# Two attention blocks on one core: the order of PE's work from a written list, part of the wide matmuls as column tiles, eps sums on GpSimd, and the last job's two copies from separate tiles

## The chip, the cores and the metric

The kernel runs on one core of a Trainium2 chip. The metric is device time of one execution in microseconds; the times given are the median of several runs. Engines are named as in the profile: PE (TensorE matmul) and PEld (its weight loads), DVE (VectorE), ACT (ScalarE), POOL (GpSimd), SP (SyncE, which issues most transfers).

## What is computed

Two attention blocks over 2048 tokens of width 640, 32 heads of 20, side by side in the output. Block A works in four segments of 512 tokens: causal softmax attention inside the segment, mixed by a gate per head with a read of a memory that earlier segments have filled. Block B is sliding-window attention (256 keys back).

```
# A, per segment s
p = softmax(qs ks^T * Dh**-0.5 + causal mask);  a_dot = p vs
num = phi(qs) M ;  den = phi(qs) z + 1e-06 ;  a_mem = num / den      # phi(t) = t+1 if t>0 else exp(t)
o = g * a_mem + (1-g) * a_dot
M += phi(ks)^T vs ;  z += sum(phi(ks))
# B
p = softmax(where(0 <= i-j < 256, q k^T * Dh**-0.5, -1e9));  o = p v
# both: out = concat over heads(o) @ wo
```

## The kernel before

**Chunks.** The work is eight chunks of 512 tokens in the order A0, B0, A1, B1, ... A3, B3, numbered n = 0 to 7. For each chunk, PE makes queries and keys (`qk_job`: ten chains of five matmuls of 512 columns), values (`v_job`: eight chains of five matmuls of 320 columns), scores, value sums and, at the end, the output projection (`final_job`: eight chains of five matmuls of 320 columns). A chain accumulates in one of two PSUM banks (`bank`, tiles m0 and m1), and a copy on DVE empties the bank (L488, L664, L669, L1014). These chains go through `wide` (L855): one matmul on the whole 128 x 128 array per step.

**Visits.** A score batch (`score_batch`, L733) fills two score tiles of three (`sc`, two banks each), with matmuls of 20 rows that run four or eight at a time as row tiles (L745). ACT turns the two tiles into `pt` by an exp each (L761). Masks follow, on POOL (`affine_select`, L800) or on DVE (multiplication with `ends`, L778). There are 153 batches. A batch can be written when the first exp of the batch before has read its tile. I call a visit what PE does from one batch to the next: the batch, then pieces of chains and, mostly, one value sum.

**Value sums.** `av` (L805, L814) and, in the last chunk, `av_tile` (L823, L835) multiply `pt` with the values of four heads in four column tiles of 32 that run side by side. Each value tile carries a column of ones, so that the sum's divisor comes out beside it. `turn` (L861) transposes the bank on DVE (L870), which frees it; `norm` (L875) takes the reciprocal of the divisor on DVE (L895) and multiplies on POOL (L905) into `o`. For A chunks after the first there is a second product for each group, the read of the memory (`mem`, L843, through `wide`). Its `norm` first adds eps to the divisor (L890, DVE), takes the reciprocal (L893), multiplies on POOL into `u` (L905) and adds `u` to `o` on DVE (L918). There are 24 of these.

**Order.** All engines run their instructions in the written order; the order is made when the kernel is built. Class `Flow` keeps a clock per engine with costs in ns for each operation. The loop in `body` (L1327 to L1422) looks at each step for what is ready by these clocks, in a fixed preference: the next score batch (L1331, not before `room`, a limit of 160 matmuls within 3000 ns, allows it, and not if ACT is far ahead and a job is ready, `may_wait`); the next value sum or memory read from the one queue `pend` (L1362, with a rule that holds it back to avoid a change of form); the next step of a job (L1387). Jobs are generators that yield what they wait for. DVE's work is put in the order of `flush`, with jobs that may wait for an idle moment (`when_idle`: the passes of phi, L523 and L529, half of the DVE masks, reciprocals, adds of `u`).

**Forms of PE.** The model in `on_pe_` charges 97 ns when the form changes ("full", "row", "row64", "col").

**End.** `final` (L928) stores `o` to DRAM and loads it back transposed for the output projection; the last chunk does this for three tiles of 128 tokens. The last 128 tokens are transposed on PE instead (`last_job`, L1023: L1036 and L1041 into the two halves of one `sc` tile), copied by DVE (L1048, 256 columns) and ACT (L1050, 384 columns) and projected by two chains (`last_half`, L1061). This job is put ahead of all others (L1476).

Of the kernel before, what the change touches and what calls it, by code (L numbers as in the profile page):

```python
# [13 lines left out]
P = 128  # L14
# [13 lines left out]
AT = 0  # L28
FETCH = 160
FETCH_NS = 3000  # L30
BACK = 800.0
NTT = 4
QPOOL = 750.0
GAP = 48
# [19 lines left out]
LEAD = 500.0  # L54

# [11 lines left out]
class Flow:  # L67
# [3 lines left out]
    def __init__(self):  # L71
# [15 lines left out]
        self.issued = []  # L87
# [11 lines left out]
    def room(self, n):  # L99


        while self.issued and self.issued[0][0] <= self.pe - FETCH_NS:
            self.issued.pop(0)
        have = n + sum(k for _, k in self.issued)
        t = self.pe
        for t0, k in self.issued:
            if have <= FETCH:
                break
            have -= k
            t = t0 + FETCH_NS  # L110
        return t

    def on_pe(self, mode, ns, cols, ready=0.0, n=1):
        self.issued.append((max(self.pe, ready), n))
        return self.on_pe_(mode, ns, cols, ready)
# [22 lines left out]
    def on_dve(self, ns, ready=0.0):  # L138
        self.dve = max(self.dve, ready) + ns
        return self.dve + 138.0  # L140

    def on_pool(self, ns, ready=0.0):
        self.pool = max(self.pool, ready) + ns
        return self.pool + 98.0
# [68 lines left out]
class _K:  # L213
# [29 lines left out]
    def warm_up(self, z):  # L243

# [211 lines left out]
    def qk_job(self, n, what, pieces, w_ap, dst, needs, scratch, phi=None):  # L456
# [6 lines left out]
        if what == "k" and self.chunks[n][0] == "B":  # L463
            at = SH
            c = self.chunks[n][1]
            if 0 in pieces and c > 0:
                def prefix(t0):
                    nc.vector.tensor_copy(out=dst[:, :, 0:SH],
                                          in_=self.kB[(c - 1) % 2][:, :, L:L + SH])
                    f.on_dve(290.0)  # L470
# [28 lines left out]
    def phi(self, in_, t, m, use):  # L499
# [13 lines left out]
        def one(in_, e, es, m, ta):  # L513
            box = []

            def s1():
# [8 lines left out]
                f.on_dve(300.0, t)  # L525

            def s2():
                r = box[-1]
                nc.vector.tensor_tensor(out=r if len(box) == 1 else e, in0=r, in1=e, op=ALU.min)  # L529
                td = f.on_dve(370.0, ta)  # L530
# [60 lines left out]
    def dm_job(self, seg, pkT, v):  # L591
# [12 lines left out]
        for some in (own, [(lambda kt, h=h: spare[:, kt, R2 * h:R2 * h + R2], R2,  # L604
# [6 lines left out]
            for lhs, rows, xs, g0 in some:  # L611
# [8 lines left out]
                f.on_pe("full", 4 * mm_ns(n), 4 * n)  # L620
# [151 lines left out]
    def mask(self, m, pt, te, ready, x):  # L772
        nc, f = self.nc, self.f
        kind, c0, n = m
        if kind == "ends":
            def go():
# [6 lines left out]
                ready[x] = f.on_dve(72.0 + 1.036 * n, te)  # L783
# [71 lines left out]
    def wide(self, ps, lhsT, rhs, n, start, stop):  # L855

        self.nc.tensor.matmul(ps[:, 0:n], lhsT=lhsT, rhs=rhs, start=start, stop=stop)  # L857
        self.f.on_pe("full", mm_ns(n), n)
        self.f.left = 0 if stop else self.KT - 1 if start else self.f.left - 1
# [15 lines left out]
    def norm(self, turned, dst, add_to, last, g=None):  # L875
# [12 lines left out]
        def s1():  # L888
            if add_to:
                nc.vector.tensor_single_scalar(out=rr[:], in_=tv[:, :, DH], scalar=EPS,  # L890
                                               op=ALU.add)
                f.on_dve(100.0, t0)
                nc.vector.reciprocal(out=rr[:], in_=rr[:])  # L893
            else:
                nc.vector.reciprocal(out=rr[:], in_=tv[:, :, DH])  # L895
            t1 = f.on_dve(276.0, t0)
            f.at(t1 - 100.0, lambda: s2(t1))

        def s2(t1):
# [14 lines left out]
            def add():  # L914
# [4 lines left out]
                t3 = f.on_dve(300.0, t2)  # L919
# [6 lines left out]
        f.when_idle(t0, s1)  # L926

    def final(self, n, o, scr, wo, out2d, r0, col, t0, t1, t):  # L928
# [19 lines left out]
        def turn(tl):  # L948
            if n not in self.oT:
# [3 lines left out]
                else:  # L953
# [7 lines left out]
                                                 lambda: box.get("t"))))  # L961
# [61 lines left out]
    def last_job(self, o, wo, out2d, r0, col, t):  # L1023
# [11 lines left out]
        for b in range(LT):  # L1035
            nc.tensor.matmul(wide[:, b], lhsT=o[:, b0 + b, 0:P], rhs=one, start=True, stop=True,  # L1036
                             skip_group_check=True)
            f.on_pe("full", mm_ns(P), P)
        for j in range(4):
            for b in range(LT):  # L1040
                nc.tensor.matmul(two[HD * j:HD * j + HD, 1, HD * b:HD * b + HD],  # L1041
# [3 lines left out]
        f.on_pe("col", 150.0, 128)  # L1045

        oT = [self.pq[:, 0, 0:2 * P], self.pkT[:, 0, 0:3 * P]]
        nc.vector.tensor_copy(out=oT[0], in_=two[:, 0, 0:2 * P])  # L1048
        td = f.on_dve(330.0, f.seen)
        nc.scalar.copy(out=oT[1], in_=two[:].rearrange("p h c -> p (h c)")[:, 2 * P:5 * P])  # L1050
        ta = f.on_act(400.0, f.seen)
        self.sc_free[own] = max(ta, td)
        yield max(ta, td)
        oT = [oT[m // 2 if m < 4 else 1][:, P * (m % 2 if m < 2 else m - 2):][:, 0:P]
              for m in range(self.KT)]
# [94 lines left out]
    def job(self, gen):  # L1150
        return [gen, next(gen)]
# [29 lines left out]
    def seed(self, n):  # L1181
# [7 lines left out]
        add = lambda gen: self.jobs.append(self.job(gen))  # L1189
# [5 lines left out]
        else:  # L1195
            add(self.dm_job(c - 1, self.pkT, self.vA))
# [7 lines left out]
        for half, pieces in enumerate(((0, 1, 2), (3, 4))):  # L1204
            for some in ([(m,) for m in pieces] if first else [pieces]):
                for what, w, dst, phi in qk:
                    need = [tx, gate] + ([self.known("wB" + what, some[0])] if first else [])
                    add(self.qk_job(n, what, some, w, dst, need, self.scr[what + kind][c], phi))
                if first and some[0] == AT:
                    add(self.late_v())  # L1210
            if first:
                v[3] = v[3] + [self.known("wBv", half)]
            add(self.v_job(n, half, *v))
# [368 lines left out]
```

## Time and profile before

| | us |
|---|---|
| median of 3 runs (lowest, highest) | 335.01 (334.55, 335.17) |
| the profiled execution | 334.66 |
| its span | 332.9 |
| granted TensorE clock | 1.0 |

| engine | busy, us | share of the span | instructions |
|---|---|---|---|
| PE | 317.7 | 95% | 6617 |
| ACT | 302.4 | 91% | 332 |
| DVE | 266.0 | 80% | 556 |
| POOL | 255.7 | 77% | 648 |

The span runs from the first to the last record of the profiled execution; that execution took 334.66 us, 1.8 us more. Busy time is the union of an engine's records. Records of matmuls overlap, and so do those of ACT: a row's mean duration is longer than the distance between two in a row. Lines such as L857 are lines of the kernel before; L857 is the helper `wide`, so its tiles tell which chain it is.

### The profile page before, as it was taken

To read this page: it belongs to the slowest core of one execution; us is meant where nothing else is said; L and a number is where in the kernel's file an instruction comes from. 1 tells how busy PE (TensorE), PEld (TensorE's weight loads), DVE (VectorE), ACT (ScalarE), POOL (GpSimd) and SP (SyncE) were. 2 spreads that over 40 slices of the span, in tenths; PEclk is the share of its full clock that TensorE was granted. 3 is DMA by queue.
4 is the path that set the end of the run, shared out by engine and by line. 5 is a ranking of instruction groups with operands and counts; after the bars stand their busy time and mean duration, and the time that the engine had idled before them with its cause. 6 is when DMAs were issued, how large, how long until landed. Compare 5 with 4: busy or idle time off the path is not lost.

```text
span 332.9 us, 15825 instructions
## 1 busy us (share of the span) xinstructions
PE 317.7 (95%) x6617; PEld 174.1 (52%) x6617; DVE 266.0 (80%) x556; ACT 302.4 (91%) x332; POOL 255.7 (77%) x648
## 2 busy tenths in 40 slices
PE   7999999999999999999999999999999999999996
PEld 2444446554444455546654546455654545666564
DVE  6878667788988899989958898888677898876653
ACT  1879999998999999999999999989999999999841
POOL 8446779987668799984876879996965969977750
PEclk9999999999999999999999999999999999999999
DMA  6975745846566852245699245044584054659762
GB/s 195 397 245 135 194 134 121 177 117 183 127 207 145 182 147 75 47 98 107 167 209 189 65 90 161 2 98 69 136 168 114 14 161 126 154 135 192 169 138 99
DMA packets 76260, 47.36 MB, mean 142 GB/s; under 512 B 48381, under 2 KB 73181, under 8 KB 76189
## 3 DMA queue, kind: packets, MB, share of 16 engines
q1 hardware_dynamic: 75469, 45.71, 56.2%
q8 instruction: 51, 0.84, 1.0%
q10 hardware_dynamic: 720, 0.66, 0.7%
q14 instruction: 20, 0.16, 0.2%
HBM read 17.62 MB, written 16.96 MB: 104 GB/s over the span
## 4 chain that ended last, share of the span: by engine, by line
PE 56%; DVE 16%; ACT 11%; POOL 7%; issue 6%; DMA 2%; SPq 1%; ACTq 0%; DVEq 0%; POOLq 0%
PE m L857 35%; PE sc L745 11%; ACT pt L761 11%; PE m L814 6%; POOL pt L800 4%; DVE pt L778 3%; PE m L835 2%; POOL u L905 2%; DVE tt L870 2%; DVE kA L488 2%; DVE pq L529 2%; DMA beta<-in_A_beta_dram 1%; DVE vA L664 1%; DVE pq L523 1%; DVE ot L1014 1%
## 5 line engine op out<-in xcount | busy, mean ns | idle before, releaser
L761 ACT ACTIVATE pt<-sc 128x1024 bf16<-128x1024 f32 (+2 forms) x306 | 284.8, 1014 | 12.4 <-PE sc L745 10.0
L800 POOL TENSOR_SCALAR_AFFINE_SELECT pt<-pt 128x128 bf16<-128x128 bf16 (+1 forms) x512 | 176.7, 373 | 62.1 <-ACT pt L761 58.4
L870 DVE STREAM_TRANSPOSE tt<-m 128x512 f32<-128x512 f32 x88 | 61.4, 711 | 20.3 <-PE m L814 9.6
L905 POOL TENSOR_TENSOR o<-tt,rr 128x320 bf16<-128x320 f32 x64 | 47.6, 743 | 4.4 <-DVE rr L895 4.1
L857 PEld LDWEIGHTS <-xT 128*128 128x128 bf16 x350 | 32.0, 97 | 25.0 <-issue 13.3
L745 PE MATMUL sc<-qB,kB 20*64 20x64 bf16 (+2 forms) x1728 | 38.6, 218 | 1.2 <-issue 0.7
L778 DVE TENSOR_TENSOR pt<-pt,ends 128x1024 bf16<-128x1024 bf16 (+2 forms) x50 | 36.0, 734 | 0.0
L745 PEld LDWEIGHTS <-kB 20*64 20x64 bf16 (+1 forms) x1728 | 21.6, 98 | 23.3 <-issue 22.0
L745 PE MATMUL sc<-qA,kA 20*64 20x64 bf16 (+4 forms) x1024 | 33.3, 237 | 0.4 <-ACT qA L485 0.2
L1014 DVE CAST ot<-m 128x320 bf16<-128x320 f32 x56 | 26.8, 485 | 7.5 <-PE m L857 7.3
L857 PEld LDWEIGHTS <-oT 128*128 128x128 bf16 x280 | 24.7, 98 | 11.4 <-issue 1.0
L857 PE MATMUL m<-wBv,xT 128*128 128x320 bf16 x160 | 27.0, 299 | 2.4 <-DVE tt L870 2.3
L857 PE MATMUL m<-wv_A,xT 128*128 128x320 bf16 x160 | 26.1, 299 | 2.6 <-DVE vA L664 1.9
L857 PE MATMUL m<-xT,wq_A 128*128 128x512 bf16 x100 | 25.8, 380 | 1.5 <-DVE vA L664 1.0
L857 PE MATMUL m<-xT,wk_A 128*128 128x512 bf16 x100 | 26.0, 388 | 1.1 <-DVE qA L488 0.7
L857 PE MATMUL m<-xT,wBq 128*128 128x512 bf16 x100 | 26.8, 381 | 0.1
L857 PE MATMUL m<-xT,wBk 128*128 128x512 bf16 x100 | 25.9, 381 | 0.0
L745 PEld LDWEIGHTS <-kA 20*128 20x128 bf16 (+1 forms) x1024 | 13.6, 97 | 20.8 <-issue 19.8
L814 PE MATMUL m<-pt,vA 128*32 128x192 bf16 (+3 forms) x512 | 23.7, 275 | 0.0
L857 PE MATMUL m<-wo_A,oT 128*128 128x320 bf16 x140 | 22.7, 300 | 0.2
L488 DVE CAST kB<-m 128x512 bf16<-128x512 f32 x20 | 13.8, 691 | 9.2 <-PE m L857 9.2
L857 PE MATMUL m<-wo_B,oT 128*128 128x320 bf16 x120 | 19.4, 300 | 0.3 <-DVE ot L1014 0.3
(108 smaller groups left out, 405.9 us busy)
## 6 DMA issues: line engine op xcount, KB each, us to landing
out_dram<-ot SPq DMA_DIRECT2D x29, 160.0 KB
scr_o<-o SPq DMA_DIRECT2D x28, 160.0 KB
xT<-in_B_x_dram SPq DMA_DIRECT2D x8, 288.0 KB
xT<-in_A_x_dram SPq DMA_DIRECT2D x8, 256.0 KB
scr_pk<-e SPq DMA_DIRECT2D x15, 128.0 KB
vS<-vA SPq DMA_DIRECT2D x16, 87.0 KB
vL<-vB SPq DMA_DIRECT2D x8, 174.0 KB
scr_kA<-kA SPq DMA_DIRECT2D x16, 60.0 KB
```

The source lines that it names most:

```text
L488: nc.vector.tensor_copy(out=dst[:, m, at:at + L], in_=ps[:, :])
L529: nc.vector.tensor_tensor(out=r if len(box) == 1 else e, in0=r, in1=e, op=ALU.min)
L745: nc.tensor.matmul(ps[j // 2][h0:h1, j % 2, c0:c0 + nq], lhsT=k[rows, g, k0:k0 + h1 - h0], rhs=q[rows, g, q0:q0 + nq], start=True, stop=Tr ...
L761: nc.scalar.activation(out=pt[:, :, lo:hi], in_=ps[i][:, :, lo:hi], func=ACT.Exp, scale=self.scale)
L778: nc.vector.tensor_tensor(out=blk, in0=blk, in1=self.ends[:, c0, :].unsqueeze(1).unsqueeze(1) .to_broadcast([P, 2, n // SH, SH]), op=ALU.mult)
L800: nc.gpsimd.affine_select(out=blk, in_=blk, pattern=pat, compare_op=ALU.is_ge, fill=self.zero, base=base, channel_multiplier=mul)
L814: nc.tensor.matmul(O[HD * j:HD * j + HD, q0:q0 + nq], lhsT=v[:, at_head(h):at_head(h) + HD], rhs=pts[j // 2][:, j % 2, c0:c0 + nq], start= ...
L835: nc.tensor.matmul(O[HD * j:HD * j + HD, o0:o0 + nq], lhsT=v[:, at_head(h):at_head(h) + HD], rhs=pts[j // 2][:, j % 2, c0:c0 + nq], start= ...
L857: self.nc.tensor.matmul(ps[:, 0:n], lhsT=lhsT, rhs=rhs, start=start, stop=stop)
L870: self.nc.vector.transpose(out=tt[:], in_=O[:, :])
L905: nc.gpsimd.tensor_tensor(out=to[:] if add_to else to, in0=a, in1=b, op=ALU.mult)
L1014: nc.vector.tensor_copy(out=ot[:, 320 * hf:320 * hf + 320], in_=ps[:, 0:320])
```

## The change

Four things change, and some costs of the planner's model with them.

1. **A list.** `PLAN` names in order what PE is given: `S` or `s` a score batch, `A` a value sum, `M` a memory read, `k20*6` six matmul steps of the job "keys of chunk 2, from piece 0", `o` an output job, `d` the memory's update, `z` the last job. The loop takes what stands next in the list, as soon as the clocks say that it is ready; the rules of preference hold only where no list is left. Memory reads have a queue of their own (`memq`) and wait for their group's value sum.
2. **Column tiles for chains.** In a visit that begins with a capital `S` and holds an `A`, `wide` issues each matmul as four, one for each 32 columns of the weights, in the form of the value sums.
3. **Eps sums.** The addition of eps to the divisor of the 24 memory reads goes from DVE to POOL (`s0`).
4. **The last job** writes its wide part (four of five pieces, 512 columns) and its tiled part (128 columns) into two `sc` tiles; DVE copies the one and ACT the other. In the list it comes last.

The model in `Flow` now charges for 256 instructions of PE in less than 3000 ns (in place of `room`), lets DVE and POOL hold each other up, and has smaller costs for phi and the adds.

```diff
+PLAN = (
+    "k00*5 q00*5 k01*4 S k01 q01*5 v00*4 s v00*14 S v00*2 k02*2 s k02*3 q02*4 S q02 k03*5 q03*5 "
...
+    "S o00*4 o10*5 S A o10*5 S o10*10 S o10*7 S o10*3 A o10*3 S o10*2 q50*5 S A q50*3 S q50*2 "
...
+    "o50*10 S A o70*5 S o60*9 A o60 S o60*5 S o60*11 S o60*9 S A o60*5 o70*5 o71*5 A o71*5 "
+    "o72*2 z0*4 ")
...
     def wide(self, ps, lhsT, rhs, n, start, stop):
-        self.nc.tensor.matmul(ps[:, 0:n], lhsT=lhsT, rhs=rhs, start=start, stop=stop)
-        self.f.on_pe("full", mm_ns(n), n)
+        f = self.f
+        if self.by_tiles:
+            for j in range(4):
+                s = slice(HD * j, HD * j + HD)
+                self.nc.tensor.matmul(ps[s, 0:n], lhsT=lhsT[:, s], rhs=rhs, start=start,
+                                      stop=stop, tile_position=(0, HD * j),
+                                      skip_group_check=True)
+            f.on_pe("col", n / 2.4 + COL_NS, n, 0.0, 4)
+        else:
+            self.nc.tensor.matmul(ps[:, 0:n], lhsT=lhsT, rhs=rhs, start=start, stop=stop,
+                                  skip_group_check=True)
+            f.on_pe("full", mm_ns(n), n)
...
-        def s1():
+        def s0():
+            nc.gpsimd.tensor_single_scalar(out=rr[:], in_=tv[:, :, DH], scalar=EPS, op=ALU.add)
+            t = f.on_pool(EPS_NS, t0)
+            f.when_idle(t, lambda: s1(t))
+
+        def s1(te=None):
             if add_to:
-                nc.vector.tensor_single_scalar(out=rr[:], in_=tv[:, :, DH], scalar=EPS,
-                                               op=ALU.add)
-                f.on_dve(100.0, t0)
                 nc.vector.reciprocal(out=rr[:], in_=rr[:])
...
-        oT = [self.pq[:, 0, 0:2 * P], self.pkT[:, 0, 0:3 * P]]
-        nc.vector.tensor_copy(out=oT[0], in_=two[:, 0, 0:2 * P])
+        oT = [self.pq[:, 0, 0:4 * P], self.pkT[:, 0, 0:P]]
+        nc.vector.tensor_copy(out=oT[0], in_=two[:, 0, :])
...
+        two = self.ps.tile([P, 2, 512], F32, name="sc", bufs=NSC)
...
-        nc.scalar.copy(out=oT[1], in_=two[:].rearrange("p h c -> p (h c)")[:, 2 * P:5 * P])
+        nc.scalar.copy(out=oT[1], in_=two[:, 0, 0:P])
...
+            want = plan[-1] if plan else None
+            self.by_tiles = bool(plan) and visits[i]
+            if i < len(bs) and want in (None, "S", "s"):
...
-                        if t <= f.pe and not self.may_wait():
+                        if t <= f.pe and (want or not self.may_wait()):
...
+                if want and jb[2] != want and (jb[2][0] != "d" or jb[1] in ("bank", 0.0)):
+                    continue
```

## Prediction, before the changed kernel had run

> **What bounds the kernel now.** I read the page first: engine shares, then the tenths by slice, then the chain that ended last.
>
> ```profile
> PE 317.7 (95%) x6617; PEld 174.1 (52%) x6617; DVE 266.0 (80%) x556; ACT 302.4 (91%) x332; POOL 255.7 (77%) x648
> ...
> PEclk9999999999999999999999999999999999999999
> ...
> q8 instruction: 51, 0.84, 1.0%
> ...
> PE 56%; DVE 16%; ACT 11%; POOL 7%; issue 6%; DMA 2%; SPq 1%; ACTq 0%; DVEq 0%; POOLq 0%
> ```
>
> PE leads the chain, ACT is close behind, and the granted clock is full throughout, so a matmul column has one price. The busy shares of both overstate them, because records overlap. The timeline of 306 to 333 us shows the true spacing:
>
> ```profile
> 305.40 7.47 ACT L761 ACTIVATE pt<-sc 128x1024 bf16<-128x1024 f32 x8
> ...
> 308.91 1.53 PE L857 MATMUL m<-wo_B,oT 128*128 128x320 bf16 x10
> ...
> 310.38 0.40 PE L745 MATMUL sc<-qB,kB 20*128 20x128 bf16 x16
> ...
> 315.41 0.34 PE L745 MATMUL sc<-qB,kB 20*128 20x128 bf16 x11 [0.74 <-issue]
> ...
> 317.15 0.40 PE L745 MATMUL sc<-qB,kB 20*128 20x128 bf16 x16
> ...
> 322.84 0.73 POOL L905 TENSOR_TENSOR o<-tt,rr 128x320 bf16<-128x320 f32 x1 [1.65 <-DVE rr L895]
> ...
> 325.40 0.48 ACT L1050 CAST pkT<-sc 128x384 bf16<-128x384 f32 x1 [2.32 <-DVE pq L1048]
> ...
> 327.57 2.26 PE L857 MATMUL m<-wo_B,xT 128*128 128x320 bf16 x15
> ```
>
> Eight exps of 1024 columns take 7.47 us, the last record 1.03: one every (7.47-1.03)/7 = 0.92 us. Ten wide matmuls of 320 columns take 1.53, a record 0.30: one every 0.136 us, 320/2.4 ns plus 2.7. The ten end their streaming at 308.91+1.36 = 310.27 and the scores begin at 310.38: a **change of form** (wide, row tiles, column tiles) costs 0.1 us. Over all changes in the trace the distance of starts, less the columns, has medians of 91 to 115 ns; I use 97.
>
> I then cut the program at its 153 visits (one score batch, then what PE does until the next). PE's own work is its columns, 2 to 4 ns a group, and 97 ns a change; ACT's is 0.833 ns a column and 52 ns an instruction. From the first score (8.66 us) to the last (317.15) there are 246.4 + 375 x 0.097 = 282.8 us of PE work and 283.9 of ACT work, and it lasts 308.5. Both engines have some 25 us to spare, in different visits: taking the longer of the two, visit by visit, gives 301.9. The other 6.6 us, and more that the visits hide, are PE waiting for PSUM banks. The waits view shows them:
>
> ```profile
> ACT pt L761 <- PE sc L745: 10.0, 24, 1.5
> DVE tt L870 <- PE m L814: 9.6, 25, 0.9
> ...
> PE m L857 <- DVE vA L664: 2.9, 5, 0.8
> ...
> PE m L857 <- DVE tt L870: 2.3, 12, 0.2
> ```
>
> ACT idles 10.0 us for scores and DVE 9.6 for value sums, so neither is the bound throughout; PE in turn waits for DVE's copies and transposes to free a bank. Matmul records hide the first 0.16 us of a wait. By distances of starts, PE's waits for DVE sum to 15.7 us: 5.5 behind transposes (L870), nearly all in the three stages with memory groups (98-137, 176-212, 254-290 us), 4.9 behind value copies (L664).
>
> **The change, part by part.** The profiled execution has a span of 332.9 us (334.66 with what lies around it); the median of the runs is 335.0, so I add 2.1 to a span.
>
> 1. *The list, forms of PE.* Built, the changed kernel has 314 changes of form against 382, and 289 wide matmuls are issued as four column tiles beside value sums. Columns are the same, 250.4 us. From first to last score: 310 changes against 375, -6.3 us; some 4.0 us of output chains come from behind the last score to ahead of it; 289 groups of four at 4 ns instead of 2.5, +0.4. Together 280.9 against 282.8: **-1.9**. The price of a group is bounded by the quartets of L814: 2.7 ns over the columns for 320, 13.3 for 448, so 0 to +3.1.
>
> 2. *The eps sums.* 24 of these leave DVE:
>
> ```profile
> L890 DVE TENSOR_SCALAR rr<-tt 128x16 f32<-128x16 f32 x24 | 8.9, 371 | 0.0
> ```
>
> 24 x 0.371 = 8.9 us of DVE, 3.0 in each memory stage, and they stand between transposes for which PE waits 5.2 us there. What goes is between none and all of that; I take half, **-2.5**. On POOL nothing has this shape; the nearest row is 128x20 at 0.23 (L338), so 24 x 0.23 = 5.5 us more. POOL is already full in part of these stages (busy 7.00 of 7 us at 123-130 and at 130-137), and behind each sum queue masks for which value sums wait. Upper bound: all 5.5 on the path; lower: 0. I take 0, since a list may place value sums later than the masks.
>
> 3. *ACT's cover.* Every visit still has two exps. The list's visits are less even: the longer of PE and ACT, visit by visit, sums to 304.9 against 301.9. A long visit after a short one is partly forgiven: the second exp (0.92) runs while PE proceeds, less score (0.2) and delivery (0.2), so half a us. I take **+1.0**, from 0 to +3.0.
>
> 4. *Instruction supply.* PE gets 867 more weight loads and as many matmuls: 14,970 against 13,236. The 51 instruction transfers are 16 KB each, one per 256 instructions. At 315.41 PE stops in the midst of a batch with nothing to wait for: 0.91 us of distance between two starts. The instructions just before were the densest stretch (370 in 6 us). In the changed list the last 35 us reach 430 to 500 by the same sums. [...] I take one more such stop, **+1.0**, from 0 to +6 (rival B).
>
> 5. *The tail.* Before, the last rows' outputs (last_job) go ahead of 15 other output matmuls, which end PE's work at 329.8; 15.75 us pass from last score to end. The list puts last_job at the end. Its chain, by rows: last score 317.15; product on POOL ends 323.57; 20 transposing matmuls 0.65; a copy of 512 columns 0.69 (row L488) with 0.24 of delivery, instead of 0.42 and 0.48 in turn (ACT's waited for DVE's, 325.40); ten groups 1.36+0.3; from there 3.0 as from the last copy at 329.87 to the end. That is 329.8 against 332.9, -3.1; PE's other work behind the last score is 5.6 us (7.45 less 1.9 of last_job), just under the 6.4 of the chain, so some of it shows. **-2.6**, from 0 to -3.5. The third tile's transposed outputs must be there: before they were issued at 320.04 and used late; the list makes their tile a visit (1.8 us) earlier and needs them about 1 us earlier.
>
> SP's transfers are moved with their stages, none is added. New separate queues for memory groups, and the waiting for the add, only order the same operations.
>
> Sum: -1.9 - 2.5 + 1.0 + 1.0 - 2.6 = **-5.0**: span 327.9, time **330.0**. The terms' ends alone reach from 324 to 343, not all at once.
>
> **Rivals.**
> A. *The waits at the stages' ends go too.* Five stops of 0.6 to 0.9 us behind value and query copies (77.9, 86.3, 143.5, 154.7, 233.4) and many smaller ones make the 10.2 us of waits for DVE outside the transposes. If the order spreads these chains, half goes: 330.0 - 5 = 325. For: ACT could follow, having 25 us to spare. Against: phi's passes on DVE, which those copies queue behind, are unchanged.
> B. *PE starves.* This is the slower side. The stop at 315.41 fits a block lasting some 4.1 us from crossing to use. If blocks drained faster than that always pay the difference, the list's dozen densest (2.6 to 3.9 us by the sums) pay 7.1 against 1.2 before, +5.9; without the gains of terms 2 and 5 that the same stretch eats half of, 332.9 - 1.9 + 1.0 + 5.9 - 2.5 = 335.4, time 337.5. It decides from where two blocks follow in under some 6 us, the last 35 us above all.
> C. *ACT sets the tempo.* The +3.0 of part 3 whole, DVE's waits unchanged because the new order only moves them: 332.9 - 1.9 + 3.0 + 1.0 - 2.6 = 332.4, time 334.5; with POOL's sums on the path up to 336.
> D. *Each added matmul has a fixed price.* By the smallest row (16 matmuls of 32 columns in 0.30 us, 8 ns apart, 4.7 over their columns): 867 x 4.7 ns = 4.1 us, time 334. [...] The trace disagrees: quartets of 64 columns start 29 ns apart, all four.
>
> **Numbers.** Forecast 0.48 (327.5 to 333), A 0.20, B 0.15, C 0.13, D 0.04. Faster by over 0.2% (0.7 us, about what a measurement here can tell from no change): forecast, A, and a little of C: 0.70. Within 0.2%: parts of C and D, 0.08. Slower: 0.22. Range 325 to 337.5, which leaves out the far ends of A and B.
>
> **What would show it.** Fewer score-to-wide changes at 97 ns and quartets of 320 columns 136 ns apart (1); waits for transposes near halved in 98-137 us (2), POOL not fuller there with masks late; ACT's idle time no larger (3); stops with "issue" in the last 35 us, none over 1 us (4); last score near 315 us and 13 us from there to the end (5). I am wrong if starved batches or late banks eat the changes saved.

## The result: 1.0% slower

| | before | after |
|---|---|---|
| median of 6 runs each, taken in turn on one chip, us | 334.38 (333.77 to 335.17) | 338.44 (334.98 to 339.23) |
| ratio, 95% interval | | 1.0101 [1.0072, 1.0129] |
| the profiled execution, us | 334.66 | 338.74 |
| its span, us | 332.9 | 336.9 |
| last score, from the span's start | 317.1 | 323.4 |
| from there to the end | 15.8 | 13.5 |

The forecast was 330.0 (325 to 337.5). The six runs of after lie further apart than those of before: the quickest, 334.98, had a granted clock of 1.0, and the profiled one, 338.74, stands near the median. Runs over 1.5% above the fastest of their kernel (three of e11's twelve below) are left out of medians and ratios. The page of after, in the same parts as shown for before:

```profile
PE 317.1 (94%) x7484; PEld 178.3 (53%) x7484; DVE 259.9 (77%) x533; ACT 300.6 (89%) x332; POOL 266.0 (79%) x672
...
PEclk9999999999999999999999999999999999998999
...
q8 instruction: 58, 0.95, 1.2%
...
PE 50%; POOL 14%; ACT 12%; DVE 9%; issue 8%; DMA 4%; SPq 1%; ACTq 0%; DVEq 0%; POOLq 0%
```

PE's busy time went down by 0.6 us, DVE's by 6.1, ACT's by 1.8; only POOL, which has the eps sums now, has 10.3 more. So the engines that led do less, in a longer span. In the last row, the chain that ended last, "issue" (time in which an engine waits for nothing that the profile shows) goes from 6% to 8% and POOL from 7% to 14%: two possible causes, both tried below. One slice of the granted clock is no longer full. The timeline of 302 to 337 us shows the first and the clock:

```profile
308.01 0.48 PE L800 MATMUL sc<-qB,kB 20*64 20x64 bf16 x37 [1.87 <-issue]
308.43 2.37 PE L921 MATMUL m<-wo_B,oT 128*128 128x320 bf16 x10
308.62 1.94 ACT L816 ACTIVATE pt<-sc 128x1024 bf16<-128x1024 f32 x2 [2.10 <-PE sc L800]
...
314.28 0.85 PE L916 MATMUL m<-wo_B,xT 128*32 128x320 bf16 x20
...
331.58 0.73 PE L916 MATMUL m<-wk_A,pq 128*32 128x320 bf16 x16 [0.62 <-DVE pq L1111]
```

In the midst of a score batch PE stands idle for 1.87 us with nothing to wait for, 2.06 from the start before to the start at 308.01. ACT runs out of scores and idles 2.10. Right behind, ten wide matmuls take 2.37 us where before they took 1.53. Twenty tile matmuls (five quartets, L916) take 0.85, so (0.85-0.30)/4 = 0.137 us from one quartet to the next, as the prediction had it. The table of stretches gives the clock's share of it; its columns are the stretch and its length, busy time and instructions of PE, PEld, DVE, ACT and POOL, granted clock, DMA share, GB/s. First before:

```profile
300.00:320.00 20.00, 19.15 (x579) 13.00 (x578) 13.36 (x28) 18.32 (x20) 15.00 (x37) 1.00 0.82 178
```

and after, for the same 20 us and for the 3.4 us behind the stop:

```profile
300.00:320.00 20.00, 17.60 (x637) 11.91 (x635) 11.23 (x25) 15.44 (x17) 13.56 (x33) 0.91 0.77 140
```

```profile
309.00:312.40 3.40, 3.40 (x29) 1.76 (x27) 2.18 (x4) 2.50 (x4) 0.00 (x0) 0.50 1.10 156
```

The clock was 0.50 for 3.4 us, which costs PE at most 1.7. Note the counts too: after asks PE for 1,272 instructions in 20 us, one block of 256 every 4.0 us. (Before asked for 1,157, one block every 4.4 us.) The waits, as "who for whom: us, times, longest", of after:

```profile
ACT pt L816 <- PE sc L800: 17.1, 27, 2.1
...
PE sc L800 <- issue: 3.4, 4, 1.9
...
DVE tt L935 <- PE m L869: 9.9, 22, 1.5
...
DVE rr L960 <- POOL rr L954: 1.4, 3, 0.6
...
PE m L921 <- DVE tt L935: 1.3, 4, 0.5
...
PE m L921 <- DVE vA L719: 0.5, 2, 0.3
```

and of before, beside the lines shown ahead of the change:

```profile
PE sc L745 <- issue: 0.7, 1, 0.7
```

ACT idles 17.1 us for scores, before 10.0; a wait of scores for "issue", 0.7 before, is now 3.4; DVE waits for value sums as before. PE's own waits for DVE became fewer: all rows of this kind add up to 5.9 us, before to 9.6. So the list did spread the chains, and what it lost it lost elsewhere.

**Where the 4.0 us are.** By the starts of the 153 batches, after is +2.4 us behind before at visit 128, +3.3 at 136, +6.3 at 152, and the tail gives 2.3 back. All stops of PE over 0.48 us between two starts that nothing releases, after the first 30 us: 0.54 (61.7), 0.68 (208.1), 1.51 (240.9), 0.66 (245.7), 0.91 (286.9), 2.06 (308.0), together 6.4 us; before has one of 0.95. Counted over all records of PE's queue (matmuls, weight loads and its few semaphore waits), **each of these stops, in both kernels, stands at record 193 modulo 256**. The pages have 58 instruction transfers of 16 KB for after's 14,985 such records and 51 for before's 13,251, one for every 258 and 260: I take a transfer to bring a block of 256, and these places for the ends of blocks.

### The profile page after: what moved, and what is told of

Read it like the earlier page. It is cut to its first block, busy times and chain, and to the rows that moved or that the text cites. A ratio compares the mean times of both kernels' runs of the same rounds, so it can differ in the third digit from the quotient of the medians.

```text
span 336.9 us, 17551 instructions
## 1 busy us (share of the span) xinstructions
PE 317.1 (94%) x7484; PEld 178.3 (53%) x7484; DVE 259.9 (77%) x533; ACT 300.6 (89%) x332; POOL 266.0 (79%) x672
## 4 chain that ended last, share of the span: by engine, by line
PE 50%; POOL 14%; ACT 12%; DVE 9%; issue 8%; DMA 4%; SPq 1%; ACTq 0%; DVEq 0%; POOLq 0%
PE m L921 23%; ACT pt L816 11%; PE sc L800 11%; PE m L916 9%; POOL pt L855 8%; PE m L869 5%; POOL o L973 2%; DVE tt L935 2%; POOL u L973 2%; PE m L890 1%; DMA beta<-in_A_beta_dram 1%; DMA xT<-scr_o 1%; DVE pt L833 1%; POOL MZ L696 1%; DMA scr_o<-o 1%
## 5 line engine op out<-in xcount | busy, mean ns | idle before, releaser
L816 ACT ACTIVATE pt<-sc 128x1024 bf16<-128x1024 f32 (+2 forms) x306 | 283.6, 1020 | 20.3 <-PE sc L800 17.1
L1085 DVE CAST ot<-m 128x320 bf16<-128x320 f32 x58 | 28.0, 484 | 13.3 <-PE m L921 10.2
L921 PEld LDWEIGHTS <-xT 128*128 128x128 bf16 x273 | 24.7, 97 | 18.1 <-issue 7.8
L800 PEld LDWEIGHTS <-kA 20*128 20x128 bf16 (+1 forms) x1024 | 13.5, 97 | 22.8 <-issue 21.7
L921 PE MATMUL m<-wBv,xT 128*128 128x320 bf16 x142 | 23.2, 299 | 1.3 <-DVE tt L935 0.5
L921 PEld LDWEIGHTS <-oT 128*128 128x128 bf16 x199 | 18.4, 100 | 10.8 <-issue 2.6
L921 PE MATMUL m<-wv_A,xT 128*128 128x320 bf16 x131 | 22.6, 300 | 1.3 <-DVE kA L543 0.8
L921 PE MATMUL m<-xT,wBk 128*128 128x512 bf16 x85 | 22.0, 380 | 0.4 <-DVE tt L935 0.3
L543 DVE CAST qB<-m 128x512 bf16<-128x512 f32 x20 | 13.7, 686 | 8.0 <-PE m L916 4.8
L921 PE MATMUL m<-xT,wBq 128*128 128x512 bf16 x78 | 19.9, 380 | 0.0
L724 DVE CAST vB<-m 128x320 bf16<-128x320 f32 x32 | 15.4, 480 | 5.4 <-PE m L916 3.6
L921 PE MATMUL m<-xT,wq_A 128*128 128x512 bf16 x77 | 19.3, 380 | 0.2 <-DVE vA L719 0.2
L973 POOL TENSOR_TENSOR u<-tt,rr 128x320 bf16<-128x320 f32 x24 | 18.1, 753 | 0.0
```

What stands on the lines that cost most here:

```text
L543: nc.vector.tensor_copy(out=dst[:, m, at:at + L], in_=ps[:, :])
L724: nc.vector.tensor_copy(out=dst, in_=src)
L800: nc.tensor.matmul(ps[j // 2][h0:h1, j % 2, c0:c0 + nq], lhsT=k[rows, g, k0:k0 + h1 - h0], rhs=q[rows, g, q0:q0 + nq], start=True, stop=Tr ...
L816: nc.scalar.activation(out=pt[:, :, lo:hi], in_=ps[i][:, :, lo:hi], func=ACT.Exp, scale=self.scale)
L973: nc.gpsimd.tensor_tensor(out=to[:] if add_to else to, in0=a, in1=b, op=ALU.mult)
L1085: nc.vector.tensor_copy(out=ot[:, 320 * hf:320 * hf + 320], in_=ps[:, 0:320])
```

## The experiments

Last score, tail (from there to the end) and stops are of the profiled execution. A stop here is a distance of over 0.48 us between two starts of PE, after the first 30 us, that stands at the end of a block of 256. The profile names a releaser for some of them: for e8's it is an exp that had ended 1.9 us earlier, and for one of 2.24 us in e11 a mask, but in after the same matmul runs without a gap, away from a block's end. "0.5 clock" says whether the clock of that execution fell to 0.5 ahead of the tail; in other executions of the same kernel it may not. The runs belong to several sessions, in which before's median was 334.34 to 334.94; the ratio is to before in the same session.

| kernel | median | ratio to before | last score | tail | stops | 0.5 clock |
|---|---|---|---|---|---|---|
| after | 338.44 | 1.0101 [1.0072, 1.0129] | 323.4 | 13.5 | 6.4 | yes |
| e1 list, eps on POOL, no tiles | 336.35 | 1.0058 [1.0039, 1.0077] | 321.3 | 13.6 | 2.0 | no |
| e2 the same, tiles to visit 95 | 336.34 | 1.0060 [1.0033, 1.0086] | 322.0 | 13.1 | 3.3 | yes |
| e12 = e2, blocks shifted | 333.65 | 0.9975 [0.9958, 0.9993] | 318.4 | 13.1 | 1.0 | no |
| e3 after, eps on DVE | 339.08 | 1.0155 [1.0122, 1.0188] | 323.5 | 13.0 | 1.5 | yes |
| e7 list, eps on DVE, no tiles | 341.23 | 1.0196 [1.0163, 1.0228] | 326.5 | 13.1 | 0 | yes |
| e8 = e7, tiles to visit 95 | 337.61 | 1.0102 [1.0067, 1.0138] | 322.7 | 13.3 | 2.1 | yes |
| e15 = e8, blocks shifted | 339.08 | 1.0124 [1.0088, 1.0159] | 325.8 | 13.1 | 0.6 | yes |
| e11 = after, shifted by 64 | 336.82 | 1.0065 [1.0040, 1.0089] | 322.7 | 13.0 | 6.6 | no |
| e16 = after, shifted by 128 | 338.04 | 1.0103 [1.0066, 1.0140] | 322.2 | 13.5 | 5.7 | no |
| e4 before, tiles | 336.62 | 1.0073 [1.0053, 1.0094] | 322.1 | 13.4 | 2.3 | no |
| e9 before, tiles to visit 132 | 334.27 | 0.9997 [0.9976, 1.0018] | 320.2 | 14.0 | 2.8 | yes |
| e13 = e9, blocks shifted | 332.81 | 0.9938 [0.9918, 0.9957] | 315.9 | 14.0 | 0.5 | no |
| e14 = before, shifted by 64 | 335.25 | 1.0029 [1.0009, 1.0048] | 317.8 | 15.9 | 1.5 | no |
| e5 before, eps on POOL | 336.90 | 1.0067 [1.0044, 1.0089] | 320.9 | 14.0 | 1.3 | no |
| e6 before, last job last | 334.97 | 1.0000 [0.9979, 1.0021] | 318.1 | 15.8 | 1.3 | no |
| e10 before, late matmuls halved | 337.70 | 1.0101 [1.0061, 1.0141] | 318.3 | 16.0 | 2.6 | no |

The theory ("supply"): PE is supplied with blocks of 256 instructions, and where a stretch uses them up faster than they come, it stops. Its rivals: the list's order itself costs the time (bank waits, ACT's cover), the eps sums on POOL cost it, or each tile matmul has a price.

**The parts of after, taken out one at a time.** e1: no tiles in the list.

```
-            self.by_tiles = bool(plan) and visits[i]
+            self.by_tiles = False
```

> The changed kernel, all of it, except that chains never go out as column tiles: every wide matmul is one instruction again (6617 matmuls, 387 changes of form against 314). Supply theory (PE ran out of instructions in the last third, and the clock dropped after the longest stop): the stops of over 0.5 us with nothing to wait for go, the clock stays at 1.0, and 73 more changes at 97 ns (7.1 us of PE work, part of it beside ACT) cost less than that: 332 to 335 us. Tempo theory (the list's uneven visits leave ACT idle, and the instructions do not matter): PE only has more to do, 339 to 343 us.

e2: tiles only where the stretch is not dense (e8 has the same line).

```
-            self.by_tiles = bool(plan) and visits[i]
+            self.by_tiles = bool(plan) and visits[i] and i < 96
```

> The changed kernel with column tiles in the first 96 of 153 visits only (to some 205 us); after that whole matmuls (7058 matmuls, 344 changes). Supply theory: all four stops of over 0.6 us lay behind 205 us; they go, and the early tiles keep their gain: 331 to 334 us, below the kernel without any tiles. Tempo theory: 338 to 341 us. If early tiles bring nothing because ACT sets the tempo there, it equals the kernel without tiles.

e3: the eps sums back on DVE, ahead of the reciprocal.

```
             if add_to:
+                nc.vector.tensor_single_scalar(out=rr[:], in_=tv[:, :, DH], scalar=EPS,
+                                               op=ALU.add)
+                f.on_dve(100.0, t0)
                 nc.vector.reciprocal(out=rr[:], in_=rr[:])
...
-        if add_to:
-            f.at(t0 - 100.0, s0)
-        else:
-            f.when_idle(t0, s1)
+        f.when_idle(t0, s1)
```

> The changed kernel with the 24 eps sums back on DVE, the rest as it is. If the eps sums on GpSimd delay masks and so value sums: 335 to 337 us, 1.5 us or more faster. If they relieve DVE as was forecast (2.5 us): 340 to 342 us. Supply theory alone, without either: within 1 us of the changed kernel, 337.5 to 339.5.

Without tiles (e1) after gains 2.1 us by the medians, 1.4 by the ratios, though it has 387 changes of form instead of 314: 73 x 97 ns = 7.1 us more of PE work, and 4.4 fewer of stops and no lowered clock. So the tiles pay for what they save with stops. But e1 met neither expectation: it is slower than supply asked (332 to 335), and two stops are left without any tile. e2 missed both as well: it was to be faster than e1 and equals it, with late stops of 1.75 and 0.75 us in a stretch that has no tiles. e3 shows that POOL's sums are not the cause: without them it is no faster.

**The parts alone, on the kernel before.** e4: wide matmuls as four tiles beside value sums, in before's order.

```
-        self.nc.tensor.matmul(ps[:, 0:n], lhsT=lhsT, rhs=rhs, start=start, stop=stop)
-        self.f.on_pe("full", mm_ns(n), n)
+        if self.f.mode == "col":
+            for j in range(4):
+                s = slice(HD * j, HD * j + HD)
+                self.nc.tensor.matmul(ps[s, 0:n], lhsT=lhsT[:, s], rhs=rhs, start=start,
+                                      stop=stop, tile_position=(0, HD * j),
+                                      skip_group_check=True)
+            self.f.on_pe("col", n / 2.4 + 3.0, n, 0.0, 4)
+        else:
...
```

> The kernel before, in which a wide matmul goes out as four column tiles whenever PE is already in the form of the value sums (7067 matmuls against 6617, 355 changes of form against 382); no list, eps on DVE, the last job as before. Column tiles alone, if they only save changes: 27 x 0.097 = 2.6 us, 332 us. Supply theory: a third more instructions in the last chunk bring stops with nothing to wait for of 1 us and more and perhaps a clock drop: 334 to 338 us.

It is 0.9 us ahead at visit 132 and 4.9 behind at 152. Between them stand two stops of 0.54 and 1.75, and 40 steps of output chains, 40 x 0.136 = 5.4 us of PE, that came behind the last score before (the tail is 2.4 shorter); part of this must be hidden, since it adds up to more than the swing of 5.8. At the end of the span it is 2.5 behind: tiles gain early and lose late.

e5: the eps sums alone on POOL (e3's edit the other way).

```
+        def s0():
+            nc.gpsimd.tensor_single_scalar(out=rr[:], in_=tv[:, :, DH], scalar=EPS, op=ALU.add)
+            t = f.on_pool(170.0, t0)
+            f.when_idle(t, lambda: s1(t))
...
-        f.when_idle(t0, s1)
+        if add_to:
+            f.at(t0 - 100.0, s0)
+        else:
+            f.when_idle(t0, s1)
```

> The kernel before with only the 24 eps sums moved from DVE to GpSimd, in the order in which the changed kernel gives them (no list, no column tiles, last job as before). The forecast's term 2: waits behind transposes shrink, 2.5 us faster, 331 to 333 us. The theory after the run with eps back on DVE (the first 280 us were 1.1 us shorter there): the sum makes masks late on GpSimd and adds two hand-overs to the divisor's chain, 335 to 336.5 us. Neither: 334 to 335.

2.0 us slower, more than either expectation. +1.0 arises at visits 96 to 104 and +2.2 between 126 and 137 us, where POOL is full (6.84 of 7 us in 130 to 137); 0.7 of that is made up by 140 us. One sum takes 280 ns on the mean, less than DVE's 371, as the row of e5 shows:

```profile
L889 POOL TENSOR_SCALAR rr<-tt 128x16 f32<-128x16 f32 x24 | 6.7, 280 | 3.0 <-DVE tt L870 0.7 <-PE m L857 0.5 <-POOL pt L800 0.3
```

and in after, 8.1 us in all against the 5.5 that I put down:

```profile
L954 POOL TENSOR_SCALAR rr<-tt 128x16 f32<-128x16 f32 x24 | 8.1, 336 | 2.5 <-DVE tt L935 0.3 <-POOL pt L855 0.3
```

e6: after's last job (two tiles, two copies), put last, in before's order.

```
-                        self.fins.insert(0, self.job(self.last_job(o, wo["end"], out2d, c * L, col, t)))
+                        self.fins.append(self.job(self.last_job(o, wo["end"], out2d, c * L, col, t)))
...
-        nc.vector.tensor_copy(out=oT[0], in_=two[:, 0, 0:2 * P])
+        nc.vector.tensor_copy(out=oT[0], in_=two[:, 0, :])
...
-        nc.scalar.copy(out=oT[1], in_=two[:].rearrange("p h c -> p (h c)")[:, 2 * P:5 * P])
+        nc.scalar.copy(out=oT[1], in_=two[:, 0, 0:P])
```

> The kernel before with only the last job changed: its two parts in two score tiles, one copy each, and the job queued behind the other output jobs instead of ahead of them. Term 5 of the forecast: the stretch from the last score to the end shrinks from 15.8 us to some 13 to 13.5: 331.5 to 332.5 us. If that stretch only shrank in the changed kernel because output chains had been moved ahead of the last score: 334 to 335.

No difference; the tail stays 15.8. after's shorter tail comes from the output chains that it places ahead of the last score, not from the last job; e4, with before's last job and chains moved ahead, has a tail of 13.4 too.

**The list alone.** e7 is e1 with e3's edit; e8 adds the early tiles.

> The changed kernel without column tiles and with the eps sums on DVE: what is left of the change is the list and the last job. If the parts add up: 336.4 for the kernel without tiles less 2.0, which the eps sums alone cost on the kernel before, 334.4, no change against the kernel before. If the list's uneven visits cost time by themselves: 336 and more. If the list is worth its sum and only the other parts spoiled it: 331 to 333.

> The list and the last job, eps sums on DVE, column tiles in the first 96 visits only: the changed kernel without the two things that the runs so far blame. If the parts add up: 336.3 less 2.0, 334.3. Best case, if a lucky order has no stop at a block's end: 332. If other waits take their place: 335 to 337.

e7 is the slowest of all, though it has the fewest new things and no stop at a block's end; it is the plainest sign that supply is not the only loss under the list. In e3 and e7 PE waits 3.0 and 2.5 us at 301 to 303 us for a transposed output tile, which neither after nor e2 does (why, e15 shows below). The parts do not add up: eps on DVE costs 0.6 with all tiles (e3 against after), 1.3 with early ones (e8 against e2) and 4.9 without (e7 against e1).

**Supply by itself.** m1 is nothing but 5,120 score matmuls of 64 columns on zeros with their weight loads, 10,240 instructions; m2 has the same beside 160 stores of 60 KB on SP.

```
        for r in range(80):
            ps = [pp.tile([P, 2, 512], F32, name="sc", bufs=3) for _ in range(2)]
            for e in range(16):
...
                    nc.tensor.matmul(ps[j // 2][h0:h0 + SH, j % 2, c0:c0 + SH],
                                     lhsT=k[rows, h0:h0 + SH], rhs=q[rows, c0:c0 + SH],
```

> Instruction supply by itself: 5120 matmuls of 20 rows and 64 columns and their weight loads (10,240 instructions, 40 blocks of 256) in the order of the masks' score batches, no transfer beside them; the attention is left out and the output is not the reference's. If a block is usable only about 3 us after the one before is entered, even with idle queues (0.9 of transfer, 1.3 from landing to use, 0.8 of request, the smallest values in the traces): about 120 us of PE. If supply keeps up with PE, 4 to 5 ns an instruction: 45 to 50 us.

> The same 10,240 instructions with 160 strided stores of 60 KB each on the SP queue beside them, of the kind that regroups queries; the output is not the reference's. If the request waits behind data packets, a block takes 4 to 5.5 us while the stores run, as in the changed kernel's stops, and 3 us afterwards: 140 us or more of PE. If data traffic does not matter: the same as without it.

m1 took 151.96 us, m2 158.65: a block takes longer than either expectation of m1 said. The timeline of m1, 60 to 80 us:

```profile
66.22 1.80 PE L102 MATMUL sc<-q,k 20*64 20x64 bf16 x128 [1.93 <-issue]
...
69.95 1.80 PE L102 MATMUL sc<-q,k 20*64 20x64 bf16 x128 [1.93 <-issue]
...
73.40 1.81 PE L102 MATMUL sc<-q,k 20*64 20x64 bf16 x128 [1.65 <-issue]
```

128 matmuls and 128 loads run in 1.80 us, and then PE stands for 1.65 to 1.93: a block starts every 3.45 or 3.73 us (up to 4.0 elsewhere in m1; 3.45 to 4.55 while m2's stores run). Against this rate stands after's 4.0 us a block over 300 to 320 us.

**The number of instructions alone.** e10 leaves before's order and forms and issues the last chunk's wide matmuls in two halves of their columns: 442 instructions more. The output of the last chunk is then not the reference's.

```
-        self.nc.tensor.matmul(ps[:, 0:n], lhsT=lhsT, rhs=rhs, start=start, stop=stop)
+        cut = (0, n // 2, n) if self.visit > 133 else (0, n)
+        for c0, c1 in zip(cut, cut[1:]):
+            self.nc.tensor.matmul(ps[:, c0:c1], lhsT=lhsT, rhs=rhs[:, c0:c1], start=start,
+                                  stop=stop, skip_group_check=True)
```

> The kernel before, its order and forms unchanged (382 changes), but in the last chunk each wide matmul is two of half the columns: 221 more matmuls and weight loads (442 instructions), the same columns, no column tiles. Supply theory: stops at the ends of blocks of 256 appear in the last 35 us, 1 us and more each, 336 to 339 us. If the number of instructions does not matter, the halves cost their 2.7 ns each: 335, no change.

3.3 us slower by the medians, with stops of 0.70, 0.67 and 1.20 at block ends in the last stage; 221 x 2.7 ns = 0.6 us is the halves' own price. The profiled execution is the fastest of its five (335.99), so the trace shows only 1.3 of the 3.3. Instructions in a dense stretch cost time, whatever form they have.

**The place of the block ends.** e9: e4's tiles where the stretch is not dense.

```
-        if self.f.mode == "col":
+        if self.f.mode == "col" and self.visit < 133:
```

> The kernel before with column tiles for a wide matmul wherever PE is in the form of the value sums, but only before the last chunk (133 of 153 visits; 6827 matmuls, 363 changes of form against 382). Supply theory: with column tiles everywhere the kernel was 0.9 us ahead at visit 132 and lost all behind it; without them in the last chunk 333 to 334 us. If column tiles do not pay at all: 334.5 to 335.5.

A miss at first: as fast as before. It is 0.5 us ahead at visit 136, and then comes the longest stop of these kernels, at 295.9 (timeline of 292 to 298 us, PE alone):

```profile
295.87 0.21 PE L745 MATMUL sc<-qB,kB 20*64 20x64 bf16 x2 [2.59 <-issue]
```

From visit 132 to 152 it has 2,211 records of PE and PEld against 2,210 in before; what differs is 210 matmuls with their loads further ahead in the stream, which move every block end behind them. That can be tried by itself: cut some of the six warm-up matmuls (512 columns on zeros, before the first score) into pieces. Everything behind them, on every engine, keeps its order and form, and the block ends move (the traces show the same order on ACT, DVE, POOL and SP with and without the pieces). The edit, with four of them in nine pieces (32 pairs of instructions more, a shift of 64; 80 pairs, 160, in e12 and e15; 72 pairs, 144, in e13; 64 pairs, 128, in e16):

```
+            if n < 4:
+                edge = [L * k // 9 for k in range(9 + 1)]
+                for c0, c1 in zip(edge, edge[1:]):
+                    self.nc.tensor.matmul(ps[:, c0:c1], lhsT=z[:, 0:P], rhs=z[:, c0:c1],
+                                          start=True, stop=True, skip_group_check=True)
+                f.on_pe("full", mm_ns(L), L)
...
```

> The changed kernel with four of the six warm-up matmuls (512 columns each) cut into nine pieces: 32 more matmuls and 32 more weight loads before the first score, the same columns, and everything behind them in the same order and form. The ends of the 256-instruction blocks move 64 instructions forward in the work. If the place of the block ends decides (each block of the trace of after held to 3.7 us from its entry to the next one's first instruction, the shortest that the idle measurement shows most often), the stops sum to 10.5 us against 3.0 at the old place: 4 to 8 us slower than the changed kernel, 342 to 346, with stops at other places than before, all at record 193 modulo 256. If only the number of instructions in a stretch counts, or if the order and forms themselves cost the time, the place makes no difference: 337.5 to 340.

> The list with column tiles before visit 96 only, and 80 more matmuls and weight loads in the warm-up (five of its matmuls cut in 17): the ends of blocks move 160 instructions forward. If their place decides, stops sum to 1.1 us by a block of 3.7 us instead of 3.8, none is near 1.7 us, and the clock stays full: 332 to 334.5, faster than the kernel before (334.4). If the list itself costs the time, 336.3 as without the shift.

> The kernel before with wide matmuls as column tiles in column form before visit 133, and 72 more matmuls and weight loads in the warm-up (six cut in 13): the ends of blocks move 144 instructions forward. If their place decides, the 2.8 us stop at 293 us goes and none over 0.9 is left: 332 to 333.5. If tiles as such gain nothing, 334.3 as without the shift.

> The kernel before with 32 more matmuls and weight loads in the warm-up (four cut in nine): the ends of blocks move 64 instructions forward. If their place decides, stops by a block of 3.7 us sum to 3.3 us instead of 0.2, the longest 1.4: 336 to 338.5. If not, 334.4 to 335.

Two hits and two misses. e13 goes from 0.9997 to 0.9938, e12 from 1.0060 to 0.9975, by nothing but a few pieces of warm-up: the place of the block ends decides where one or two long stops are all there is. e13 is faster than both kernels. The misses: e14 is slower, but by 0.5 us where 1.5 to 4 were expected, and e11 is not slower than after at all: its stops come to 6.6 us, as many as after's, and its clock stays full. My reckoning (every block held to 3.7 us from entry to the next) is too simple to give sizes: blocks pass without a stop in as little as 2.3 us in e11, and take up to 5.5 at a stop in after.

> The changed kernel with 64 more matmuls and weight loads in the warm-up (four of its matmuls cut in 17): block ends moved 128 instructions forward, a third place beside after (338.4) and e11 (337.7). If the dense last 35 us, with tiles in every stage, has too many instructions for any place, it pays some 4 us in stops here too: 336 to 339. If a good place alone is missing, one of the three should show it: under 335.

> The list with eps sums on DVE and column tiles before visit 96 only, with the same 80 pieces in the warm-up as e12: the same instructions of PE as e12, the eps sums alone on the other engine. Without the pieces it took 337.6, with a stop of 2.1 us and a lowered clock behind it. If the stops' place decides, none over 1 us is left and the clock stays full: 332 to 335, and its distance to e12's 333.65 is what the eps sums' engine is worth under the list (term 2 of the prediction: DVE 2.5 slower, 336.1; the opposite, as in the kernel before alone: DVE 2.0 faster, 331.7). If the list costs the time, 337.6 again.

e16: a third place, 338.04, with stops of 2.56, 0.90 and 1.13 late. (35 matmul records are missing in its trace, and its late stops stand at record 158, which with 35 is 193.) So of after, three places give 338.4, 336.8 and 338.0, with 6.4, 6.6 and 5.7 us of stops: with tiles in the last stage the stream is too dense for any of the three.

e15 is a miss of another kind: only one short stop is left, and yet it is 5.4 us slower than e12, which has the same PE instructions in the same order. Its timeline, 290 to 306 us:

```profile
291.84 3.27 SPq L1012 DMA_DIRECT2D scr_o<-o  x4
...
295.21 3.19 SPq L1031 DMA_TRANSPOSE oT<-scr_o  x1
...
302.37 0.85 PE L931 MATMUL m<-wo_B,oT 128*128 128x320 bf16 x5 [3.08 <-DMA oT<-scr_o]
```

and that of e12:

```profile
289.54 2.72 SPq L1036 DMA_TRANSPOSE oT<-scr_o  x1
```

The list names PE's order only; SP's follows from the planner's clocks. With the eps sums on DVE these put the store of the next output tile (`scr_o<-o`, four issues, 3.27 us of SP) ahead of the transposition, and with them on POOL behind it. So the transposition is issued 5.7 us later, PE waits 3.1 us for it, and then runs 3.4 us at a clock of 0.5. e3, e7 and e8 have the same order on SP; in e8 the 2.1 us stop stands just ahead of the use and covers the wait, and when the shift took the stop away in e15, the wait took its place. It explains the last part of e15's distance; 3.3 us of it are there at visit 136 already, and stay unexplained.

## Why the prediction was wrong

**Term 4, instruction supply, is the step that failed.** I put +1.0 us ("one more such stop", an estimate from the one at 315.41), with 0 to +6 as bounds. It measured 6.4 - 0.95 = +5.4 of stops, and up to 1.7 of lowered clock behind the longest, which no term held: up to +7.1. (My counts of 14,970 and 13,236 are 14,968 and 13,234 on the pages.) The stop at 315.41 in before was the sign of it, and the densest blocks were listed in rival B, which I gave 0.15. B was what happened: it said +5.9 and 337.5. Its place was only half right: 3.4 us of the stops come before visit 132, at 61, 208, 241 and 246 us. Late stops alone are 3.0 against 0.95, so that B's size came out near is in part luck.

The books of the profiled executions:

| | forecast | measured |
|---|---|---|
| 1 PE's own work | -1.9 | -1.9 (by the same sums: 280.9 against 282.8; not measured by itself) |
| 2 and 3, eps sums and ACT's cover | -2.5 + 1.0 | +1.1 or more, what is left |
| 4 supply, with the clock | +1.0 | up to +7.1 |
| 5 tail | -2.6 | -2.3 |
| sum | -5.0 | +4.0 |

*Term 1*'s price was right, with the quartets at 0.137 us, and the result shows that PE's work is no measure of the time here. *Term 2* was of the wrong sign for the edit alone (+2.0 in e5, -2.5 forecast): POOL was as full as I had read, and I took 0 for its end of the range because a list "may place value sums later". In after, PE's waits for transposes did shrink (2.3 to 1.3 us by the view's largest row), as the term said, but DVE's transposes wait for POOL's masks 3.9 us instead of 1.3. Under the list, the opposite edit is never faster (e3, e8, e7, e15), so POOL is the right engine there, but not for the term's reason: the 5.4 us of e15 against e12 hold a transposition that SP issues late, and a lowered clock. *Term 3*: ACT's idle time for scores rose by 7.1 us instead of staying, though the stops, 5.4 us more, probably make up most of that. *Term 5* was right in size, but not for the reason that the step led with: the last job alone is worth 0.0 (e6); the chains moved ahead of the last score make the tail shorter, and they are paid for there.

Rival D (a fixed price for each added matmul, 4.1 us) is not needed: e13 has 210 more matmuls than before behind its warm-up, and is faster. Rival C had the sign but not the size (334.5, at most 336), and its mechanism was not seen: ACT is starved and does not set the tempo. Of what I said would show it, the quartets and the tail came; no stop over 1 us, ACT's idle time unchanged and a last score near 315 did not.

Only 6 of after's 58 crossings show a stop, and the six cost more (6.4 us) than terms 1 and 5 brought together (4.2). In m1 each crossing from 60 to 80 us shows one, of 1.65 to 1.93 us.

**What stays open.** What decides whether a given block stops: entry to next takes from 3.35 to 5.5 us at after's stops, and the block's transfer begins anything from 0.8 to 2.9 us after entry; beside m2's stores a block took up to 4.55 us, in m1 up to 4.0, but I have no rule for it. Nor is the rest of the list's loss settled: at a good place and with one stop, e12 still has its last score 1.2 us later than before; e7 has no stop and is the slowest. And no place tried frees after itself of its stops, so what it would take without them is not shown.

## What to carry to other kernels

Divide the instructions of the densest stretch into its time: where a block of 256 is used up in under some 4 us (a block took 3.45 to 4.0 us in m1), cutting a matmul in four can cost more than the change of form that it saves, so put such tiles where the stream is thin and leave the dense end alone (e13: 0.6% faster; at another place of the block ends, e9, no faster). A stop with "issue" in the middle of a batch is the sign; count PE's records to it, and if it stands at a block's end, a few more pieces of warm-up move it; whether to a better place has to be tried (e14 lost 0.3% by it). Test the parts of a change together as well as alone: here an order found with the sums on one engine was up to 5 us slower with them on the other.

## What the runs showed of the hardware

- All stops of PE over 0.48 us that nothing releases (six in after, one in before, after the first 30 us) stand at record 193 modulo 256 of its queue. At full use a block of 256 takes 3.45 to 4.0 us with idle queues (m1), up to 4.55 beside stores (m2). At the stops PE goes on 1.29 to 1.62 us after the block's transfer has ended (after; 1.19 to 1.58 in m1).
- After some stops the clock falls to 0.5, for 3.4 us in after (309.0 to 312.4 us): in the profiled executions after ones of 1.75 us (e2), 2.06 (after), 2.1 (e8), 2.8 us (e9), and after waits for data of 2.5 to 3.2 us (e3, e7, e15); the mean granted clock of these seven was 0.993 to 0.995. It did not after 1.75 in e4, 2.24 in e11 or 2.56 in e16 (mean clock 1.0), so the stop's length alone does not decide it. What does was not shown.
- What a drop costs shows in e9: its five runs at a granted clock of 0.993 to 0.995 took 335.26 us on the mean, its seven at 1.0 took 333.82.
- A shift of the block ends by 144 or 160 instructions, with the work unchanged, moved two kernels by 0.6% and 0.8%, as much as e4's or e5's edit (0.7%).
